# Attention plus feed-forward on one core: a four-sum seven-product form, reciprocals kept in PSUM, GpSimd casts in quarters, other PSUM rings, and stores issued by ScalarE

## The chip, the cores and the metric

The kernel runs on 1 core of one Trainium2 chip. The metric is device microseconds of one execution; lower is better. A profiled execution also has a span, from its first to its last instruction, which lies some 2 us under its time.

In the profile's lines PE is TensorE, DVE VectorE, ACT ScalarE, POOL GpSimd and SP SyncE; a q behind the name (SPq) means its queue of issues, and L194 is line 194 of the kernel. Tiles named _ps lie in banks of PSUM, one of the chip's two kinds of on-chip memory used here, and take TensorE's products; all other tiles lie in SBUF, the other kind.

## The reference, cut to what matters

There are two softmax attentions in a row, then a feed-forward layer whose weights serve all batches. 512 of the 576 tokens of a batch are "main" tokens; the other 64 are the "remainder", which the kernel collects over four batches into one "remainder unit".

```python
# q, k, v: (8 batches, 8 heads, 576, 64); p: (8, 8, 32, 64)
p_packed = softmax(p @ k.T / 8) @ v             # 32 packed rows per head
out      = softmax(q @ p_packed.T / 8) @ p_packed
x = out.transpose(0, 2, 1, 3).reshape(4608, 512)
h = x @ w_in                                    # 512 -> 2048
g = h * sigmoid(beta * h)
y = g @ w_out                                   # 2048 -> 512
```

## The kernel before

The program orders itself: every piece of work is a task with an engine, a duration, its dependencies and a rank, and a planner lays the tasks out in time once, when the program is built. The order found is fixed in each engine's queue. In the tile names, h_ps, o_ps and w_ps are PSUM banks of h, of the output and of a batch's fused weights W_bf (p_packed times w_in, scaled; h is then one product of the second softmax with them); hr_ps is h of the remainder; g_main is g, which ScalarE makes with the activation called silu here.

For one output unit (256 tokens by 512 outputs) `g @ w_out` is done as seven products of half blocks instead of eight. VectorE makes the sums, TensorE the products into four PSUM banks, ScalarE and VectorE gather them in `o_sb`, and SyncE stores them:

```python
# sums: 3 instructions, 5 blocks of 128x1024
S[0:2] = g[0:2] + g[2:4];  S[2] = g[0] + g[3];  g[1:3] = g[1:3] - g[0:4:3]
# banks: C = A11*w3 | A22*w4,  D = S5*w5 | S2*w2,  A = S7*w7 | S6*w6,  B = S1*w1
# takes: copy of C on ScalarE, then subtract D, add D, add A, add B on VectorE
...
def store(self, unit):
    if unit[0] != "r":                                   # main unit: one store
        nc.sync.dma_start(rows[:, 2 * v : 2 * v + 2, :], o[:])
    else:                                                # remainder unit: four
        for e in range(4):
            nc.sync.dma_start(self.out[lo : lo + SR, :], o[64 * (e % 2) : ..., e // 2, :])
```

The second softmax's sums are inverted by ScalarE as exp(-ln z), out of PSUM into an SBUF tile `rz2`, from which VectorE multiplies:

```python
nc.scalar.activation(rz[:, i, 0:SM], ps[:], AF.Ln)       # PSUM -> SBUF
nc.scalar.activation(rz, rz, AF.Exp, scale=-1.0)         # in SBUF
nc.vector.tensor_tensor(A2T, E2T, rz, ALU.mult)
```

The rings of PSUM banks are 2 for h, 3 for the output, 3 for attention.

The softmax here doesn't subtract the row's maximum and nothing guards it: scores larger than these inputs give would overflow.

## Time and profile before

| | before |
|---|---|
| time, median of 3 runs | 261.63 us (261.55 to 262.82) |
| span of the profiled execution, granted clock | 259.1 us, 0.998 |
| TensorE, VectorE, ScalarE, GpSimd busy | 93, 77, 68, 24% |

The profiled execution took 260.84 us, less than all three timed runs.

This is the timeline of SyncE (start, length, queue, line, operation, count):

```profile
167.79 1.27 SPq L250 DMA_DIRECT2D k32r<-in_k_dram  x2
169.10 0.61 SPq L242 DMA_DIRECT2D v<-in_v_dram  x1
169.81 2.56 SPq L809 DMA_DIRECT2D out_dram<-o_sb  x4
```

The view of waits (who waited for whom: total us, times, longest) says that stores hold this queue for long, and that silu (L639) hardly ever holds TensorE:

```profile
SPq L805 <- DVE o_sb L782: 55.5, 7, 14.3
...
PE h_ps L194 <- ACT g_main L639: 0.6, 3, 0.2
```

A store at the head of SyncE's queue waits for VectorE's last addition, up to 14.3 us, and all loads behind it wait too. That is what moving the stores to another engine aims at. SyncE computes nothing, so its waiting only matters when a load becomes late.

### The profile page before, as it was taken

To read this page: it belongs to the slowest core of one execution; us is meant where nothing else is said; L and a number is where in the kernel's file an instruction comes from. 1 tells how busy PE (TensorE), PEld (TensorE's weight loads), DVE (VectorE), ACT (ScalarE), POOL (GpSimd) and SP (SyncE) were. 2 spreads that over 40 slices of the span, in tenths; PEclk is the share of its full clock that TensorE was granted. 3 is DMA by queue.
4 is the path that set the end of the run, shared out by engine and by line. 5 is a ranking of instruction groups with operands and counts; after the bars stand their busy time and mean duration, and the time that the engine had idled before them with its cause. 6 is when DMAs were issued, how large, how long until landed. Compare 5 with 4: busy or idle time off the path is not lost.

```text
span 259.1 us, 6793 instructions
## 1 busy us (share of the span) xinstructions
PE 241.7 (93%) x2897; PEld 193.8 (75%) x2897; DVE 199.2 (77%) x288; ACT 176.1 (68%) x308; POOL 63.4 (24%) x58
## 2 busy tenths in 40 slices
PE   4899689899989999998999999999999999999990
PEld 4897576566554878886778877877889778889880
DVE  6476766887985987796888968979996688665771
ACT  1153579867877878879786987886898768765000
POOL 4320433151440741342315231600900000000000
PEclk9999999999999999999999999999999999999999
DMA  7999999997998998996998999989660102201113
GB/s 225 352 320 268 280 325 384 348 330 183 288 199 237 292 246 235 212 333 148 265 251 263 143 318 291 205 227 272 174 172 7 79 0 83 82 27 60 81 81 81
DMA packets 73471, 54.18 MB, mean 209 GB/s; under 512 B 42065, under 2 KB 66657, under 8 KB 73441
## 3 DMA queue, kind: packets, MB, share of 16 engines
q1 hardware_dynamic: 73440, 53.76, 75.2%
q8 instruction: 22, 0.36, 0.6%
q14 instruction: 9, 0.07, 0.1%
HBM read 37.23 MB, written 9.44 MB: 180 GB/s over the span
## 4 chain that ended last, share of the span: by engine, by line
PE 56%; DMA 20%; SPq 10%; ACT 4%; issue 3%; POOL 3%; DVE 2%; POOLq 0%
PE o_ps L194 31%; PE h_ps L194 14%; DMA k<-in_k_dram 9%; SPq L336 5%; DMA v<-in_v_dram 4%; PE w_ps L194 3%; DMA qT<-q_bf 3%; SPq L250 2%; PE hr_ps L194 2%; DMA q32r<-in_q_dram 2%; DMA v32r<-in_v_dram 2%; PE z_ps L194 2%; PE s_ps L194 1%; SPq L242 1%; ACT g_main L639 1%
## 5 line engine op out<-in xcount | busy, mean ns | idle before, releaser
L639 ACT ACTIVATE g_main<-h_ps 128x512 bf16<-128x512 f32 x128 | 71.1, 596 | 29.5 <-PE h_ps L194 28.6
L194 PE MATMUL h_ps<-A2T,W_bf 128*128 128x256 bf16 x512 | 70.2, 273 | 0.6 <-ACT g_main L639 0.6
L194 PEld LDWEIGHTS <-W_bf 128*128 128x128 bf16 x768 | 57.1, 98 | 12.7 <-issue 4.7
L194 PE MATMUL o_ps<-w_mix,g_main 128*128 128x256 bf16 x448 | 59.5, 273 | 0.0
L194 PEld LDWEIGHTS <-g_main 128*128 128x128 bf16 x512 | 48.2, 98 | 12.5 <-issue 2.9
L600 DVE TENSOR_TENSOR W_bf<-w_ps,beta_bc 128x512 bf16<-128x512 f32 x64 | 41.5, 682 | 5.7 <-PE w_ps L194 5.2
L194 PEld LDWEIGHTS <-g_sums 128*128 128x128 bf16 x384 | 36.4, 98 | 5.5 <-issue 1.4
L209 ACT ACT_TABLE_LOAD x28 | 35.9, 1283 | 1.2 <-PEq L1067 0.7
L194 PE MATMUL o_ps<-w_out_bf,g_sums 128*128 128x256 bf16 x256 | 33.9, 273 | 0.0
L707 DVE TENSOR_TENSOR g_sums<-g_main 128x2048 bf16<-128x2048 bf16 x14 | 21.8, 1555 | 4.8 <-ACT g_main L639 4.8
L194 PE MATMUL warm_ps<-identr 128*128 128x128 bf16 x256 | 21.9, 237 | 3.7 <-DVE bones L858 3.7
L276 POOL CAST q_bf<-q 128x2048 bf16<-128x2048 f32 (+1 forms) x7 | 14.6, 2081 | 33.5 <-DMA q<-in_q_dram 19.9
L194 PEld LDWEIGHTS <-identr 128*128 128x128 bf16 x256 | 18.0, 108 | 5.5 <-DVE bones L858 3.7
L276 POOL CAST v_bf<-v 128x2048 bf16<-128x2048 f32 (+1 forms) x7 | 13.4, 1912 | 26.2 <-PE h_ps L194 9.8
L774 DVE TENSOR_TENSOR o_sb<-o_sb,o_ps 128x512 f32<-128x512 f32 x16 | 11.0, 685 | 10.0 <-ACT g_main L639 2.5
L541 DVE TENSOR_TENSOR A2T<-E2T,rz 128x512 bf16<-128x512 bf16 (+1 forms) x24 | 13.6, 587 | 5.5 <-ACT rz L536 5.5
L276 POOL CAST k_bf<-k 128x2048 bf16<-128x2048 f32 (+1 forms) x7 | 12.4, 1771 | 21.4 <-DMA k<-in_k_dram 10.4
L711 DVE TENSOR_TENSOR g_main<-g_main 128x2048 bf16<-128x2048 bf16 x14 | 17.4, 1244 | 0.0
L194 PE MATMUL o_ps<-w_mix,g_sums 128*128 128x256 bf16 x128 | 17.3, 273 | 0.0
L194 PE MATMUL o_ps<-w_out_bf,g_main 128*128 128x512 bf16 x64 | 17.0, 380 | 0.0
L772 ACT COPY o_sb<-o_ps 128x512 f32<-128x512 f32 x16 | 9.4, 588 | 10.3 <-PE o_ps L194 10.2
L194 PEld LDWEIGHTS <-pp 64*32 64x32 bf16 x384 | 6.0, 88 | 13.5 <-issue 10.9
(86 smaller groups left out, 296.5 us busy)
## 6 DMA issues: line engine op xcount, KB each, us to landing
out_dram<-o_sb SPq DMA_DIRECT2D x16, 512.0 KB, 3.9
k<-in_k_dram SPq DMA_DIRECT2D x7, 1024.0 KB, 8.5
v<-in_v_dram SPq DMA_DIRECT2D x7, 1024.0 KB, 6.8
q<-in_q_dram SPq DMA_DIRECT2D x7, 1024.0 KB, 6.7
w_in<-in_moe_w_in_dram SPq DMA_DIRECT2D x4, 1024.0 KB, 9.4
w_out<-in_moe_w_out_dram SPq DMA_DIRECT2D x4, 1024.0 KB, 12.4
k<-in_k_dram SPq DMA_DIRECT2D x2, 512.0 KB, 5.4
k32r<-in_k_dram SPq DMA_DIRECT2D x16, 64.0 KB, 5.2
```

The source lines that it names most:

```text
L194: return self.nc.tensor.matmul(out, lhsT, rhs, start=start, stop=stop, tile_position=pos, skip_group_check=True)
L209: self.nc.scalar.preload_act_table_set(SETS[mode])
L250: nc.sync.dma_start(t[64 * g : 64 * g + 64, :].rearrange("p (h d) -> p h d", h=4), src[b, 4 * g : 4 * g + 4, SM:S, :].rearrange("h p d -> ...
L276: self.copy[engine](self.t[b, x][:, 0:2048].rearrange("p (t h d) -> p h t d", t=4, h=8)[:, h], self.t[b, x, "32"][:].rearrange("p (h t d) ...
L336: nc.sync.dma_start_transpose(t[:], st[b, x][:])
L541: nc.vector.tensor_tensor(part(st[b, "A2"], i), part(st[b, "E2"], i), part(st[b, "rz2"], i), ALU.mult)
L600: nc.vector.tensor_tensor(st[b, "W"][:, r, cols], st[b, "w", m][:], self.beta_bc[:, cols], ALU.mult)
L639: nc.scalar.activation(st[b, v, "g"][:, :, f, :], st[b, "h", v, f][:].rearrange("p (q n) -> p q n", q=4), AF.Silu)
L707: nc.vector.tensor_tensor(st[*unit, "S"][:, 0:2], g[:, 0:2], g[:, 2:4], ALU.add)
L711: nc.vector.tensor_tensor(g[:, 1:3], g[:, 1:3], g[:, 0:4:3], ALU.subtract)
L772: nc.scalar.copy(middle, st[*unit, "C"][:])
L774: nc.vector.tensor_tensor(ends, middle.rearrange("p (h n) -> p h n", h=2)[:, ::-1], halves(st[*unit, "D"]), ALU.subtract)
```

## The change

It has seven parts: (1) four sums and seven products that accumulate in two banks, with reads in the middle; (2) the second softmax's reciprocals stay in PSUM; (3) the first softmax's reciprocal is applied per partition, to the exponent and to W_bf; (4) GpSimd casts in pieces of 128x512; (5) PSUM rings 3 for h, 2 for output, 3 for attention; (6) q of the first two batches has staging of its own; (7) the first 16 units are stored by ScalarE, and the planner's order is retuned with 1119 per-task offsets. Besides, one unit instead of two is done with plain products, and the second remainder unit now comes before the last main unit.

In the diff, cut to its core, the lines of sums, steps, casts and reciprocals are condensed.

```diff
+STORE_US = 5.0
+STORE = 'ACT'
+RINGS = {'h': 3, 'o': 2, 'att': 3}
+OFFSETS = {0: 10.1, 1: 4.7, 2: 101.3, ...}              (1119 entries, cut)
...
     def add(self, engine, us, fn, deps=(), rank=0, ...):
+        rank += OFFSETS.get(len(self.tasks), 0)
...
-                self.copy[engine](to, of)
+                m = 2 if engine == "POOL" else n
+                for j in range(0, n, m):
+                    self.copy[engine](to[:, j : j + m], of[:, j : j + m])
...
-            nc.scalar.activation(rz[:, i, 0:SM], ps[:], AF.Ln)
-            nc.scalar.activation(rz, rz, AF.Exp, scale=-1.0)
-            nc.vector.tensor_tensor(A2T, E2T, rz, ALU.mult)
+            nc.scalar.activation(sums(i), sums(i), AF.Ln)
+            nc.scalar.activation(sums(i), sums(i), AF.Exp, scale=-1.0)
+            nc.vector.tensor_tensor(A2T, E2T, sums(i), ALU.mult)
...
+        0: S0 = a21 + a22;  1: S1 = S0 - a11;  2: S2 = a12 - S1;  3: a21 = a11 - a21
+        steps = a21*B21 -> bank 1, a11*B11 -> bank 0, S0*T1 -> bank 1, S1*T2 -> bank 0,
+                S2*B22 -> bank 1, a12*T3 -> bank 0, a22*T4 -> bank 0    (a take between two)
...
+    def plan_store(self, unit, deps):
+        e = STORE if len(self.outs) < 17 else "SP"
+        us = {"POOL": 1.0, "ACT": 0.5, "SP": 1.5}[e]
+        self.task(("store", unit), e, us, lambda: self.store(unit, e), deps, -10)
+
-    def store(self, unit):
+    def store(self, unit, engine):
+        dma = {"POOL": self.nc.gpsimd, "ACT": self.nc.scalar, "SP": self.nc.sync}[engine].dma_start
```

The planner takes a store on ScalarE for 0.5 us of that engine. Here the store of the first remainder unit, four transfers, is among the 16 units that ScalarE stores.

## The prediction

> **What bounds the kernel now.** I read, in this order, the page's busy row and slices, the stretches of 10 us, the chain, and the timelines of the start and of the end.
>
> ```profile
> PE 241.7 (93%) x2897; PEld 193.8 (75%) x2897; DVE 199.2 (77%) x288; ACT 176.1 (68%) x308; POOL 63.4 (24%) x58
> ...
> DMA  7999999997998998996998999989660102201113
> ```
>
> TensorE (PE) looks like the bound, but the ends of matmuls are modelled, so I take its pace from the chain:
>
> ```profile
> 198.27 3.06 PE o_ps L194 x28
> ...
> 237.83 15.30 PE o_ps L194 x140
> ```
>
> Both lines (start, length, what) give 0.109 us for a matmul of 128x256. In the same way a 512-wide one of the plain output takes 0.218 us (two in 0.43), an hr_ps one 0.029 (32 in 0.93), a w_ps one 0.043 (eight in 0.34), a pp_ps one 0.029 (20 in 0.58). With these I weigh all matmuls of the built program, fillers (warm_ps, identity products that only keep PE busy) left out: 212.7 us of real work in a span of 259.1. The other 46.4 us are what can be won. Where are they? The timelines show:
>
> ```profile
> 46.13 0.41 PE L194 MATMUL w_ps<-w_in_bf,pp 64*32 64x512 bf16 x8
> ...
> 44.49 1.59 POOL L975 CAST w_in_bf<-w_in 128x1024 bf16<-128x1024 f32 x1 [1.26 <-DMA w_in<-in_moe_w_in_dram]
> ```
>
> At 46.13 PE starts the last column block of batch 0's fused weights, which needs the last quarter of w_in, landed at 44.49 and cast until 46.08. I use this as the anchor. Before it PE does 212.7 - 197.2 = 15.5 us of real work, so 30.6 us of the 46.4 lie there, spent on loads. After it 197.2 us of work are left (488 h and 896 output products of 0.109 = 150.7; 64 plain of 0.218 = 13.9; small ones 32.6) and PE ends at about 253.15, 207.0 later: 9.8 us of gaps, of which stretch counts put about 2.8 before 60, 4.1 between 60 and 130, and 2.5 after that. The last 5.9 us are the end:
>
> ```profile
> 253.15 0.69 DVE L782 TENSOR_TENSOR o_sb<-o_sb,o_ps 128x512 f32<-128x512 f32 x1 [0.19 <-PE o_ps L194]
> 253.87 2.46 SPq L809 DMA_DIRECT2D out_dram<-o_sb  x4
> ```
>
> One addition, then four stores issued one after the other, and their landing.
>
> The start is a matter of loads. SyncE's queue (SPq) issues them in order, and it stood still twice:
>
> ```profile
> 13.11 1.06 SPq L242 DMA_DIRECT2D q<-in_q_dram  x1
> 19.26 0.37 SPq L242 DMA_DIRECT2D k<-in_k_dram  x1
> 19.73 1.28 SPq L250 DMA_DIRECT2D k32r<-in_k_dram  x2
> 21.05 1.27 SPq L250 DMA_DIRECT2D q32r<-in_q_dram  x2
> 22.73 0.37 SPq L242 DMA_DIRECT2D v<-in_v_dram  x1
> 28.08 0.37 SPq L242 DMA_DIRECT2D q<-in_q_dram  x1
> ```
>
> Nothing is issued from 14.2 to 19.26 and from 23.1 to 28.08, because k, v and q share two staging buffers. In the stretches the rate is 324, 255, 336 and 379 GB/s from 10 to 50 us: the dip from 20 to 30 follows these stops.
>
> **What the Trainium skill says.** "TensorE: Matmul & The Clock Gate", section "Back-to-back issue gap", gives 262 cycles at 2.4 GHz for 256 columns, which is 109 ns: the trace agrees. The same section's sustained 131 ns for 512 columns does not hold here, 218 ns does. "SBUF — State Buffer", section "Who interferes with whom", says that a VectorE instruction with two SBUF inputs contends with a GpSimd instruction that reads SBUF. The trace agrees:
>
> ```profile
> 85.42 1.89 POOL L276 CAST v_bf<-v 128x2048 bf16<-128x2048 f32 x1 [9.76 <-PE h_ps L194]
> ...
> 85.69 2.69 DVE L707 TENSOR_TENSOR g_sums<-g_main 128x2048 bf16<-128x2048 bf16 x1
> ```
>
> The sum takes 2.69 us beside a cast, and 1.22 after 190 us, where GpSimd is idle. "PSUM — Partial Sum Buffer", section "The four PSUM rules", allows a synchronised read of a partial sum in the middle of an accumulation; the new form lives on that, and no run of before shows it. "DMA: Bandwidth & Descriptors", section "Issuing engines are not separate DMA queues", says that issuing from another engine saves only sequencer time, so I count nothing for stores on ScalarE (ACT) as transfers.
>
> **The change part by part.**
>
> PE: only the first unit of outputs stays plain instead of two. 32 matmuls of 0.218 = 6.97 become 56 of 0.109 = 6.10: -0.9 us. The first softmax's sums are 80 products with one moving column; I estimate 0.029 each, the pace at which hr_ps loads weights, against 0.040 now: -0.9 us. Total work 210.8 against 212.7. But the order of the built program, counted from the same anchor, leaves 197.7 us after it (492 and 952 of 0.109 = 157.3; 32 of 0.218 = 7.0; 33.4 small), not less than 197.2: batch 1's q is loaded after w_in now, so its transposes and scores, and some h, move behind the anchor. The saved PE work therefore shows only in front, where PE idles anyway. This is the central step: **PE work after the anchor: +0.5 us.**
>
> Loads: q of batches 0 and 1 gets its own staging, so k and v of batch 1 wait only for the casts of k and v of batch 0. Counted from the SyncE order, about 12.1 MiB stand up to the last w_in, against 12.2 before. If the stretch from 20 to 30 us moves at the neighbours' 330 GB/s instead of 255, it carries 0.75 MB more, worth 2.3 us. The cast behind it goes in two halves of estimated 0.6. **Anchor: -2 us.**
>
> VectorE (DVE): the sums become four of 128x1024 (0.685 each beside an idle GpSimd) for 17 units, 46.6 us, against 61.2 now (21.8 + 17.4 + 15.8 + 6.2 for the remainder units). With GpSimd's casts in quarters a sum meets at most about 0.6 us of cast, not 1.89, so I add some 4 us. The 128x128 reciprocals fall from 8 x 0.952 to 8 x about 0.16 (-6.3). The normalisation falls from 16 x 0.287 to 8 x about 0.42 (-1.2). One w_mix operation less: -1.3. Evictions: 102 of 128x256 at an estimated 0.42 (0.685 less the 256 columns at 0.96 GHz) = 42.8, against 43.6 + 2.7. W_bf gets a second factor: 64 x 0 to 0.06 = up to +3.8. Sum: 199 to about 179. DVE isn't the bound, so this is worth only shorter gaps.
>
> ACT: 16 copies of 0.588 become 17 of about 0.38 (-3), and 19 store issues come on its queue, at the 0.6 that one costs on SPq (+11). Both kernels load 28 tables. ACT stays near 75%; the danger is that a store at its head waits for an eviction and holds up silu.
>
> Buffers: three banks for h let PE run one product further ahead of silu, which aims at the handshake near 50 us, where ACT and PE alternate with 0.2 us waits. Two for o with reads in the middle of accumulations mean that two steps on the same bank need an eviction between them, about 0.2 + 0.42 + 0.2; another step of 8 x 0.109 = 0.87 fits into this, except before the last unit's last step: +0.7. The reciprocals hold their bank for some 2 us. I expect **gaps: -2.5 us** of the 9.8, mainly before 130 us, and **tail: -0.4 us**: +0.7 as said, and -1.1 because the last unit is now a main one, with one store instead of four.
>
> Sum: +0.5 - 2 - 2.5 - 0.4 = -4.4. As the order was retuned task by task, which works on exactly these gaps, I lean 1 us further: 261.6 - 5.4 = 256.2.
>
> **Rivals.**
>
> (1) The anchor doesn't move. Loads are in flight in nearly every slice up to 190 us, the same bytes are wanted, and the two stops may be hidden by the backlog. For it: 1.05 to 1.09 of DMA share. Against: the dip to 255 GB/s. Then 258 to 260.
>
> (2) A new wait eats the gain. Batch 1's q arrives behind w_in and w_out, and its softmax comes after batch 0's silu; PE has 17.4 us of listed work between the anchor and batch 1's first h, against my count for ACT of 13 silus (7.2), a table load (1.3) and a softmax (5 to 6) with its hops: just enough. If PE has to wait there, or stores block ACT, the result is 259 to 263.
>
> (3) The gaps nearly vanish and the loads come faster still: gaps at 4 us and the anchor at 43 make 259.1 - 3.1 + 0.5 - 5.8 - 0.4 = 250.3 of span, 252.8 as time (the median lies 2.5 above the span). For it: after 130 us the old order already loses only 2.5 us in 123.
>
> **Range and chances.** The sum's terms are uncertain by about 2 us (anchor), 2.5 (gaps) and 1 (tail, stalls), together some 3.4 us: 8 in 10 within 251.3 to 260.8. The 2% line is at 256.4, just above my number, so faster by over 2% and the same are close; slower than 266.9 would take a new serial wait of 10 us, for which I see nothing.
>
> **What would show it.** Right: last w_in cast ending near 44 instead of 46.08; PE's last product near 249; gaps of some 7 us after the anchor; 128x1024 sums near 0.75 on average; one store after the last addition; DVE near 180 us busy. Wrong: the anchor at 46 or later (loads), PE waits named ACT or a q transfer between 50 and 65 us (rival 2), or matmul pace other than 0.109 in the unit products because they wait on evictions.

## The result, and the profile after

| | before, same rounds | after |
|---|---|---|
| median | 262.14 us, 4 runs | 269.06 us, 4 runs (268.44 to 271.89) |
| ratio, 95% interval | | 1.0284 (1.0205 to 1.0363): slower |
| span and clock of the profiled execution (before: the earlier one) | 259.1 us, 0.998 | 267.3 us, 0.987 |

A ratio is the mean time of one kernel's fast runs over that of the other's fast runs of the same rounds, so it isn't quite the ratio of the medians beside it. Executions over 1.5% slower than the fastest of the same kernel are left out of the means.

The page of the changed kernel: busy row, then three rows of 40 slices (6.7 us each).

```profile
PE 242.8 (91%) x2915; PEld 196.9 (74%) x2915; DVE 176.9 (66%) x335; ACT 172.9 (65%) x309; POOL 70.2 (26%) x119
...
PE   4988789999799999999999999099999999999992
...
ACT  1136544863998897998798984094898898653000
...
PEclk9999999999999999999999999869999999999999
```

In slice 25 (counted from 0: 167 to 174 us) both TensorE and ScalarE show 0, and the granted clock drops to 8 and then 6 tenths in this slice and the next. One hole, not a general slowness. ScalarE's timeline across it (in brackets: how long the engine was idle before, and what ended it):

```profile
162.80 0.60 ACT L749 ACTIVATE g_main<-h_ps 128x512 bf16<-128x512 f32 x1
168.41 4.66 ACTq L919 DMA_DIRECT2D out_dram<-o_sb  x4
173.11 1.57 ACT L749 ACTIVATE g_main<-h_ps 128x512 bf16<-128x512 f32 x3 [9.72 <-DMA q<-in_q_dram]
```

ScalarE's last silu ends at 163.40. Then the four stores stand at the head of its queue: the first goes out at 168.41, the last at 172.59, and only then silu goes on. The bracket doesn't name an eviction by VectorE, it names the load of q. SyncE's timeline has that load and the ones before it:

```profile
160.51 1.42 SPq L365 DMA_DIRECT2D v32r<-in_v_dram  x2
162.02 1.38 SPq L365 DMA_DIRECT2D k32r<-in_k_dram  x2
164.82 0.37 SPq L357 DMA_DIRECT2D q<-in_q_dram  x1
```

Why should a store of o_sb wait for a load of q? The built program says it. Every transfer issued by SyncE or ScalarE reports its landing on one of eight semaphores (counters that instructions can wait for), which the build hands out in program order across both queues, and before an issue a queue waits until the transfer that had this semaphore last has landed. For the four stores:

```
store   semaphore   had it last (issued by SyncE)   waits besides for
1       DMAHW0      v32r, second half               VectorE's take
2       DMAHW1      k32r, first half                -
3       DMAHW2      k32r, second half               VectorE's take
4       DMAHW3      q, 1 MB                         -
```

VectorE's takes are not what held them: the two named in the table had ended at 161.43 and 164.96 in the trace, before ScalarE was free for the first store (163.40) and before the third one's turn (169.59). The chain of waits confirms the last row to 0.02 us (start, length, what):

```profile
164.82 7.75 DMA q<-in_q_dram
172.57 0.02 issue
172.59 0.47 ACTq L919
...
175.20 1.71 PE o_ps L295 x8
...
177.33 1.59 PE hr_ps L295 x32
```

The q load is issued at 164.82 and lands 7.75 us later, at 172.57; the fourth store goes out at 172.59. The last two lines show a second cost: eight matmuls of 128x256 take 1.71 us, 0.214 each instead of 0.109, and 32 hr_ps 1.59 us instead of 0.93. After its idle time TensorE is granted a mean clock of 0.66 in the 10 us from 170 on.

The Trainium skill states both halves of this. "DMA: Bandwidth & Descriptors", section "Anatomy of one DMA — SWDGE (gpsimd) path", a section on GpSimd's transfers, notes that "any semaphore wait happens on the issuing sequencer before dispatch", and "Perfetto Trace Analysis", section "Tensor Engine Instruction (MATMUL, LD_WEIGHTS)", notes that "ACT/DVE/GPSIMD are strict FIFO". The trace agrees with both: 9.72 us during which silus wait behind a store.

TensorE's timeline at the anchor, at the hole, and at the end:

```profile
44.73 0.96 PE L295 MATMUL w_ps<-w_in_bf,pp 64*32 64x512 bf16 x8 [0.27 <-POOL w_in_bf L1088]
...
173.76 1.01 PE L295 MATMUL h_ps<-A2T,W_bf 128*128 128x256 bf16 x4 [6.62 <-ACT g_main L749]
...
261.92 1.03 PE L295 MATMUL o_ps<-w_mix,g_main 128*128 128x256 bf16 x8 [0.51 <-DVE o_sb L877]
```

I count TensorE's gaps in the way of the prediction, as a stretch less its matmuls at their paces. The third column is the first experiment, below, in which only those four stores are back on SyncE:

| stretch | before | after | rem_sp |
|---|---|---|---|
| anchor to 60 us | 2.8 | 1.8 | 2.4 |
| 60 to 75 | 0.7 | 2.3 | 2.4 |
| 75 to 150 | 4.1 | 3.5 | 3.3 |
| 150 to 190 | 1.2 | 10.1 | 1.2 |
| 190 to TensorE's end | 0.9 | 2.9 | 2.6 |
| sum | 9.7 | 20.5 | 11.7 |

Of the 10.1 us from 150 to 190, 6.62 are the wait itself; 1.5 more are the low clock behind it, in the two groups just shown (1.71 and 1.59 us instead of 0.87 and 0.93). A part of the change that works as intended is seen in the groups of instructions (count, busy us, mean ns, then idle time before):

```profile
L830 DVE TENSOR_TENSOR g_sums<-g_main 128x1024 bf16<-128x1024 bf16 x15 | 11.1, 737 | 2.6 <-ACT g_main L749 2.1
```

The sums meet short casts only: 737 ns on average for this form. Before, one of 128x2048 took 2.69 us beside a long cast and 1.22 without.

### The profile page after: what moved, and what is told of

Same layout as the page of the kernel before. It is cut to its first block, busy times and chain, and to the rows that moved or that the text cites.

```text
span 267.3 us, 6970 instructions
## 1 busy us (share of the span) xinstructions
PE 242.8 (91%) x2915; PEld 196.9 (74%) x2915; DVE 176.9 (66%) x335; ACT 172.9 (65%) x309; POOL 70.2 (26%) x119
## 4 chain that ended last, share of the span: by engine, by line
PE 58%; DMA 22%; SPq 6%; DVE 5%; POOL 3%; issue 2%; ACT 1%; ACTq 1%; POOLq 0%; DVEq 0%
PE o_ps L295 32%; PE h_ps L295 16%; DMA w_out<-in_moe_w_out_dram 6%; DMA w_in<-in_moe_w_in_dram 4%; DMA qT<-q_bf 4%; SPq L365 3%; DMA q<-in_q_dram 3%; DMA v32r<-in_v_dram 3%; PE hr_ps L295 3%; PE w_ps L295 3%; DMA k<-in_k_dram 2%; PE s_ps L295 2%; SPq L357 2%; PE z_ps L295 1%; SPq L1076 1%
## 5 line engine op out<-in xcount | busy, mean ns | idle before, releaser
L710 DVE SCALAR_TENSOR_TENSOR W_bf<-w_ps,rz,beta_bc 128x512 bf16<-128x512 f32 x64 | 45.3, 744 | 21.4 <-PE w_ps L295 21.3
L295 PE MATMUL o_ps<-w_out_bf,g_main 128*128 128x256 bf16 (+1 forms) x272 | 39.2, 285 | 0.9 <-DVE o_sb L879 0.5
L877 DVE TENSOR_TENSOR o_sb<-o_sb,o_ps 128x256 f32<-128x256 f32 x51 | 21.2, 418 | 24.1 <-PE o_ps L295 23.5
L295 PE MATMUL o_ps<-w_mix,g_sums 128*128 128x256 bf16 x272 | 36.6, 277 | 0.2
L295 PE MATMUL o_ps<-w_mix,g_main 128*128 128x256 bf16 x240 | 33.1, 273 | 0.5 <-DVE o_sb L877 0.5
L879 DVE COPY o_sb<-o_ps 128x256 f32<-128x256 f32 x51 | 21.3, 420 | 16.8 <-PE o_ps L295 15.1
L395 POOL CAST q_bf<-q 128x512 bf16<-128x512 f32 x26 | 17.3, 706 | 46.0 <-DMA q<-in_q_dram 25.3
L395 POOL CAST k_bf<-k 128x512 bf16<-128x512 f32 x26 | 15.8, 652 | 21.2 <-DMA k<-in_k_dram 13.9
L395 POOL CAST v_bf<-v 128x512 bf16<-128x512 f32 x26 | 16.8, 686 | 11.6 <-PE h_ps L295 3.1
L295 PE MATMUL o_ps<-w_out_bf,g_sums 128*128 128x256 bf16 x136 | 18.8, 273 | 0.0
```

The costliest lines, as they stand in the source:

```text
L295: return self.nc.tensor.matmul(out, lhsT, rhs, start=start, stop=stop, tile_position=pos, skip_group_check=True)
L395: self.copy[engine](to[:, j : j + m], of[:, j : j + m])
L710: nc.vector.scalar_tensor_tensor(st[b, "W"][:, r, cols], st[b, "w", m][:], st[b, "rz1"][:, r : r + 1], self.beta_bc[:, cols], ALU.mult, AL ...
L877: nc.vector.tensor_tensor(o, o, ps, ALU.add)
L879: self.copy[engine](o, ps)
```

## The experiments

The theory (A) after the first reading: the time is lost because the four remainder stores wait on ScalarE for SyncE's loads, and silu with them. The rivals: (1) it is the change of store engine as a whole, wherever the stores stand; (2) the new arithmetic and buffers have made something else slower. All kernels gave correct results. This is the overview; "before" is measured again in each batch.

| run | median us of its fast runs | ratio to before | 95% interval |
|---|---|---|---|
| rem_sp | 258.94 | 0.9866 | 0.9790 to 0.9942 |
| rem_sp_again | 259.42 | 0.9914 | 0.9861 to 0.9968 |
| rem_pool | 260.65 | 0.9965 | 0.9874 to 1.0055 |
| rem_two | 265.19 | 1.0079 | 0.9997 to 1.0160 |
| before_rem_act | 270.50 | 1.0329 | 1.0277 to 1.0381 |
| before_all_act | 271.68 | 1.0323 | 1.0232 to 1.0413 |
| all_sp | 265.43 | 1.0102 | 1.0008 to 1.0196 |
| all_pool | 272.84 | 1.0367 | 1.0290 to 1.0444 |
| rem_sp_prime | 259.85 | 0.9901 | 0.9810 to 0.9993 |
| rz_sbuf | 264.30 | 1.0096 | 1.0023 to 1.0169 |
| whole | 260.20 | 0.9922 | 0.9869 to 0.9975 |
| untuned | 266.21 | 1.0170 | 1.0115 to 1.0226 |

### rem_sp: the four stores back on SyncE

```diff
     def store(self, unit, engine):
+        engine = "SP" if unit[0] == "r" else engine
```

> The changed kernel in its planned order, only the four stores of the first remainder unit are issued by SyncE instead of ScalarE. Theory A: these four stores stood at the head of ScalarE's queue from 163.4 to 173.1 us, waiting on DMA semaphores held by SyncE's loads (the last one by a 1 MB load of q), and so held up silu and PE. Then the wait of 9.7 us on ScalarE and the PE gap of 6.6 us vanish: 259 to 261 us. Theory B: batch 7's k and q land late and PE would starve there whatever issues the stores: 266 us or more. DMA bytes and PE work are the same in both.

258.94 us, just under what I expected; the profiled execution has span 258.0, clock 0.995. The same three silus now start at 165.29 instead of 173.11, and the stores go out on SyncE at 172.22:

```profile
165.29 1.57 ACT L749 ACTIVATE g_main<-h_ps 128x512 bf16<-128x512 f32 x3 [1.92 <-PE h_ps L295]
...
172.22 3.40 SPq L920 DMA_DIRECT2D out_dram<-o_sb  x4
```

TensorE loses 1.2 us between 150 and 190 instead of 10.1, and nothing else was touched. One added line makes the difference between 2.8% slower and 1.3% faster than before (0.9% in the second measurement, rem_sp_again).

### before_rem_act: the remainder's stores moved alone, in the kernel before

```diff
-                nc.sync.dma_start(self.out[lo : lo + SR, :], o[64 * (e % 2) : ..., e // 2, :])
+                nc.scalar.dma_start(self.out[lo : lo + SR, :], o[64 * (e % 2) : ..., e // 2, :])
```

> The kernel before with nothing but the two remainder units' stores (four each) issued by ScalarE at their old places; main stores stay on SyncE. Theory A (the four stores at the head of ScalarE's queue wait for SyncE's loads that went eight transfers earlier, and silu with them): a wait of ScalarE of 3 us or more near 168 to 173, a PE gap of 3 to 4.5 us behind it, and 265 to 267 against some 262.5. Theory B (it is the main stores on ScalarE that cost the time in before_all_act): within 1 us of before, and no such wait.

270.5 us: 8 us lost by one word, more than expected. The word moves the second remainder unit's four stores too; the loss is at the first unit's: TensorE's gaps from 150 to 190 are some 9 us larger than before. ScalarE's and TensorE's timelines:

```profile
166.41 5.53 ACTq L809 DMA_DIRECT2D out_dram<-o_sb  x4
171.98 1.08 ACT L639 ACTIVATE g_main<-h_ps 128x512 bf16<-128x512 f32 x2 [8.78 <-DMA k32r<-in_k_dram]
...
172.63 1.01 PE L194 MATMUL h_ps<-A2T,W_bf 128*128 128x256 bf16 x4 [7.87 <-ACT g_main L639]
```

Again the bracket names a load. It is the last of four waits: by the issues and landings in the trace the first store waited for a main store of SyncE (landed at 166.33), the second for a transposition (169.70), the other two for halves of k32r (the last landed at 171.44). VectorE's last addition had ended at 161.98, before ScalarE's wait began at 163.2. None of the new arithmetic and none of the new buffers is in this kernel, so rival (2) isn't needed for the loss.

### before_all_act: all stores on ScalarE, in the kernel before

```diff
-            nc.sync.dma_start(rows[:, 2 * v : 2 * v + 2, :], o[:])
+            nc.scalar.dma_start(rows[:, 2 * v : 2 * v + 2, :], o[:])
     (and the four of the remainder as in before_rem_act)
```

> The kernel before in its order, with all stores issued by ScalarE instead of SyncE: one part of the change alone. Theory A: ScalarE's head waits on SyncE's loads through the shared DMA semaphores; silu and PE stop as in the changed kernel: 266 to 275 us, with waits of ScalarE of several us in front of its stores. Rival: ScalarE is busy only 68% and takes stores without harm, 261 to 263 us, and the loss of the changed kernel needs its new order.

271.68 us, as theory A expected. Its ratio, 1.0323, is that of before_rem_act, 1.0329. TensorE waits 4.43 us at 174.13, behind the remainder's stores, and 3.07 us at 125.80, behind a main store that waited on ScalarE for a load of k32r. So a main store can be held in the same way; the sum isn't larger than with the remainder's alone.

### rem_two: two stores for the four

```diff
+            rows = self.out.rearrange("(b s) n -> s b n", s=S)[SM:S, 4 * unit[1] : 4 * unit[1] + 4]
+            if unit[1] == 0:
+                for r in range(2):
+                    dma(rows[:, r::2, :], o[64 * r : 64 * r + 64, :, :])
+                return
```

> The changed kernel with the first remainder's four stores on ScalarE as it has them, but merged into two. In the built program the two wait only on the DMA semaphores DMAHW0 and DMAHW1, which in the changed kernel's trace were free at 168.4 and 169.0 us; the third and fourth, which waited for 169.9 and for the 1 MB load of q until 172.6, are gone. Theory A (each store waits for the DMA that used its semaphore last): ScalarE is released some 3.5 us earlier, the wait falls from 9.7 to about 6 us, 265 to 266.5 us. Rival (ScalarE waits for the evictions of the unit or for the issue of the stores itself): released at about the same time or one issue earlier, 268 to 269 us.

With two stores only two semaphores are needed. ScalarE goes on at 169.84 instead of 173.11:

```profile
169.84 1.57 ACT L749 ACTIVATE g_main<-h_ps 128x512 bf16<-128x512 f32 x3 [6.69 <-DVE g_main L830]
...
170.49 0.78 PE L295 MATMUL h_ps<-A2T,W_bf 128*128 128x256 bf16 x4 [3.27 <-ACT g_main L749]
```

The bytes stored are the same, the wait is 6.69 us instead of 9.72, and the time is about 3.9 us shorter (medians of different batches); the expectation of theory A held. The bracket names VectorE, whose work only happened to end last before silu: the first store went out at 168.44, when the second half of v32r had landed at 168.37, and the second was issued until 169.80. What sets the wait is which earlier transfer each store has to see landed, not the size of the stores.

### rem_pool: the four stores on GpSimd

```diff
+        engine = "POOL" if unit == ("r", 0) else engine
```

> The changed kernel with the first remainder unit's four stores issued by GpSimd at the same place of the plan, all else as it is; GpSimd's stores use semaphores of their own in the built program and wait only for VectorE's evictions. Theory A (ScalarE's wait was for SyncE's loads, through the shared semaphores): no wait of ScalarE near 163 to 173, PE gap there under 1 us, and 258.5 to 261, as in rem_sp. Theory B (four stores at this place cost the time on any queue of a computing engine): GpSimd's casts come late, k's transposition and the next batch's scores with them, a PE gap of 3 us or more between 165 and 200, and 264 or more.

In the built program GpSimd's stores have semaphores of their own. Its timeline:

```profile
169.85 0.40 POOL L398 CAST k_bf<-k32r 128x256 bf16<-128x256 f32 x1 [5.73 <-DMA k32r<-in_k_dram]
170.40 2.20 POOL L920 DMA_DIRECT2D out_dram<-o_sb  x4
```

The stores go out even at 170.40, behind a cast that waits for its load, and cost nothing: TensorE loses 1.0 us between 150 and 190. The median of its three fast runs, 260.65, lies in the 258.5 to 261 expected, and the profiled span is 258.5, beside 258.0 of rem_sp. Theory B of this run fails. With so few runs the interval holds 1: that this version beats before isn't shown.

### all_sp: all stores on SyncE

```diff
+        engine = "SP"
```

> As the last one, but all stores are issued by SyncE, order of the plan kept. Theory A: as without the four stores, and the first store on ScalarE, which took 3.5 us to issue, is gone too: 257 to 260 us. Rival: SyncE now stands at its head until evictions are done (it did for 55 us in the kernel before), loads and transposes come later, and new PE gaps open: 262 to 266 us.

My expectation failed, the rival's range held: 265.43. Main stores on SyncE do wait at the head for VectorE (60.2 us in nine waits). But the longest waits of TensorE are not for late loads. VectorE's and TensorE's timelines show one:

```profile
114.86 0.42 DVE L879 COPY o_sb<-o_ps 128x256 f32<-128x256 f32 x1 [2.81 <-DMA out_dram<-o_sb]
...
115.33 1.03 PE L295 MATMUL o_ps<-w_mix,g_sums 128*128 128x256 bf16 x8 [2.21 <-DVE o_sb L879]
```

A store that SyncE issued at 105.33 landed 9.4 us later, at 114.76, and until then VectorE couldn't write that o_sb again. In rem_sp ScalarE issued this store at 104.67, and it landed after 5.1 us. TensorE's wait of 2.20 us at 171.18 is of the same kind (8.3 us to land). Why a store lands later from SyncE's queue, no run settles. So this order, which was made for stores on ScalarE, is slower without the 15 main stores there, and faster only without the remainder's.

### all_pool: ScalarE's stores on GpSimd

```diff
+        engine = "POOL" if engine == "ACT" else engine
```

> All stores that ScalarE issues in the changed kernel are issued by GpSimd at the same places of the plan. The built program shows that these stores have semaphores of their own (DMASW) and wait for evictions alone. Theory A: no wait of ScalarE or PE near 163 to 173 us, time as with the four stores on SyncE, 257.5 to 260 us. Rival 1: GpSimd's casts stand behind stores that wait for evictions, so k and q are late and PE waits for transposes: 261 to 265 us. Rival 2: the loss near 167 us is due to late loads after all: 266 us or more.

272.84 us. Theory A and rival 1 failed; the time lies in the range of rival 2, but not for its reason. The wait near 163 to 173 is gone, but the timelines of GpSimd, VectorE and TensorE show another one earlier:

```profile
143.86 0.53 POOL L916 DMA_DIRECT2D out_dram<-o_sb  x1
...
149.17 0.43 DVE L879 COPY o_sb<-o_ps 128x256 f32<-128x256 f32 x1 [9.02 <-DMA out_dram<-o_sb]
...
149.65 1.01 PE L295 MATMUL o_ps<-w_mix,g_sums 128*128 128x256 bf16 x4 [8.43 <-DVE o_sb L879]
```

The store stands in GpSimd's queue behind the casts of k, which began at 141.63 after 3.38 us of waiting for k. It goes out at 143.86, lands at about 149.1, and only then VectorE may write that o_sb again, and TensorE the PSUM bank. It is the mirror of the first case: a queue that waits for loads makes stores late, as a store that waits makes a queue late.

### rem_sp_prime: an earlier first transfer on ScalarE's queue

In rem_sp too, ScalarE's first store is strange; every other one takes 0.34 to 0.40 us (where this store is the first transfer on ScalarE's queue, the other runs of the new kernel show 3.2 to 4.8):

```profile
63.34 3.53 ACTq L916 DMA_DIRECT2D out_dram<-o_sb  x1
```

The edit issues beta's load from ScalarE at the very start:

```diff
+        self.b16 = self.const.tile([16, 128], f32, name="b16")
+        nc.scalar.dma_start(self.b16[:], self.beta.rearrange("(f p) -> f p", p=128))
...
-            nc.sync.dma_start(self.b16[:], self.beta.rearrange("(f p) -> f p", p=128))
```

> The four stores on SyncE, and beta's small load moved to ScalarE's queue at the very start, so that this queue's first DMA is no longer a store at 63 us. If the 3.5 us of that first issue belong to the first use of the queue: the issue at the start takes the 3.5 us while ScalarE has nothing to do, the first store takes 0.34 us, and the time falls 1.5 to 3 us below the run without it (257 to 259). If the 3.5 us are a wait on a load: the first store still takes over 2 us and the time is the same within 1 us.

The long issue disappears (0.37 us at 63.56; beta's at the start takes 0.40, not 3.5), but the time doesn't fall: TensorE then waits 1.88 us at 69.99 for k's transposition. And in before_all_act the first store of ScalarE took 0.38 us without any such preparation. So what makes it 3.5 us stays open, and taking it away alone gained nothing.

### rz_sbuf: the reciprocals in SBUF again

```diff
-            nc.scalar.activation(sums(i), sums(i), AF.Ln)
+            if i == 0:
+                st[b, "rz2"] = self.one.tile([128, 2, S], f32, tag="rz2", name="rz2")
+            nc.scalar.activation(part(st[b, "rz2"], i), sums(i), AF.Ln)
     (the exponential and the product from rz2 too; on top of rem_sp)
```

> The four stores on SyncE, and the reciprocals of the second softmax's sums written to SBUF as in the kernel before instead of staying in PSUM. One part undone, order kept. Expected: ScalarE's exponentials on them go from about 580 to 630 ns, the product A2T on VectorE contends with GpSimd's casts again (0.69 to about 0.74 us), both off the path: within 1 us of the run without it (258 to 260 us). If the part is worth something by itself, 261 us or more.

A miss: 264.3, where I expected rem_sp's time within 1 us. The same stores of ScalarE, found in both timelines, show where it comes from: the second is 1.2 us later than in rem_sp, the seventh (144.52 against 143.60) 0.9 later, the eighth (160.46 against 157.31) 3.2 later, the last 3.9 later. So up to the eighth store the part costs the expected 1 us. The chain has the step at the eighth:

```profile
151.62 8.77 DMA kT<-k_bf
160.38 0.02 issue
160.40 0.02 ACTq L919
```

This store has to wait until k's transposition has landed, which had the store's semaphore last. It is the theory's wait once more, now in a main store: ScalarE was free at 158.36 and VectorE's take was done at 158.03, so the wait is 2.0 us of the 4.0 by which the spans differ (262.0 against 258.0). The store then lands at 168.13, and VectorE and TensorE (1.48 us at 169.03) wait for that. Why the transposition is issued over 6.79 us here and 3.99 in rem_sp, I couldn't settle.

### whole: GpSimd's casts uncut

```diff
-                m = 2 if engine == "POOL" else n
+                m = n
     (and w_in's cast in one piece; on top of rem_sp)
```

> The four stores on SyncE, and GpSimd's casts whole again instead of in quarters. Expected: the 128x1024 sums on VectorE rise from 0.74 us on average to about 0.9, GpSimd's busy time falls by some 8 us, PE's gaps change little: 258 to 260 us. If the quarters matter for PE, the gaps after 60 us grow by 2 us or more: 261 us or more.

The time, 260.2, is as expected. The sums get longer on the whole, though less than I wrote (means of 813, 690 and 794 ns against 727, 739 and 719 in rem_sp), GpSimd is 57.6 us busy against 71.8, VectorE 180.3 against 177.1. The medians differ from the two of rem_sp by 1.3 and 0.8 us; that the quarters are worth anything isn't shown.

### untuned: without the table of offsets

```diff
-        rank += OFFSETS.get(len(self.tasks), 0)
```

> rem_sp (the changed kernel with the first remainder unit's four stores on SyncE) with the table of about 1200 per-task offsets left out, so that the planner orders the same instructions by its own ranks. Theory A, the prediction's step: the retuning is worth about 1 us beside the change's own parts, so this takes 259.5 to 261.5 and is still about 0.5 to 1% faster than before. Theory B: what rem_sp gains over before is the tuned order, and the parts by themselves bring little: then 263 or more, with new PE gaps of 2 us and over in the trace, at waits that rem_sp doesn't have.

266.21 us: my step was too small, theory B held. Without the table the same instructions take 6.8 us more (median) than in rem_sp_again of the same batch. TensorE's largest wait falls behind ScalarE's first store:

```profile
70.97 1.32 PE L294 MATMUL h_ps<-A2T,W_bf 128*128 128x256 bf16 x8 [3.12 <-ACT g_main L748]
```

The gaps from 60 to 75 are 5.2 us (2.4 in rem_sp), and all those after 75 add up to 11.4 (7.0 in rem_sp).

### rem_sp_again: the best version in five rounds

> rem_sp once more, unchanged, in five rounds. If it beats the kernel before by what the first measurement showed, the ratio lies at 0.983 to 0.991 with an interval that excludes 1; if that was a chance of three rounds, the interval reaches 0.995 or more.

The ratio is 0.9914, at the edge of what I wrote, and the interval (0.9861 to 0.9968) excludes 1 but not 0.995. This kernel beats before and the changed kernel. Over both measurements the gain against before is about 1%, less than the 2% that count as faster.

Not run: the new form with the old rings of 2, 3 and 3 banks. With the table of offsets the planner finds no order for it; without the table it builds, and could have been compared with untuned. So what the rings bring by themselves stays open, as does the new form against the old with all else equal.

## Why the prediction was wrong

**The step that failed** is the one on ScalarE: "19 store issues come on its queue, at the 0.6 that one costs on SPq (+11) ... the danger is that a store at its head waits for an eviction and holds up silu". The cost of an issue was even overstated: most took 0.34 us. The danger was seen, but the cause of the wait was looked for in the wrong place: evictions account for none of it. The four stores of the first remainder unit wait for the landing of four loads of SyncE, up to 7.75 us after issue, because the built program's eight semaphores are shared by both queues. For this ScalarE stood 9.72 us and TensorE 6.62. rem_sp, before_rem_act, rem_two and rem_pool show it from four sides; in before_rem_act the four waits were for a store, a transposition and two loads of SyncE. It could have been read before the run: the changed kernel can be built, and each store's waits stand in the built program. I looked only at the order of the instructions.

**The reading of the skill.** "I count nothing for stores on ScalarE (ACT) as transfers" was right for the bytes and led astray for the queue. Rival (2) did name "or stores block ACT", with 259 to 263. The blocking was shown, at 269. The sentence on a slowdown over 266.9, "would take a new serial wait of 10 us, for which I see nothing", came near the size: the wait is 9.72 us on ScalarE. The reading of the matmul page was too narrow: beside the 131 ns that don't hold, the same section gives 518 cycles for 512 columns, 216 ns, which do.

**The anchor** was expected 2 us earlier and came 1.4 us earlier (46.13 to 44.73; 44.66 in rem_sp). But part of this is the cast in halves: the first two of the eight products now start after the first half. Like with like, the last w_in cast ends at 45.24 instead of 46.08 (predicted: near 44) and starts at 43.54 instead of 44.49, so the loads brought 0.9 us, under half of the step. Nor does it come from the stretch named: from 20 to 30 us the rate rose from 255 to 301 GB/s, but from 10 to 20 it fell from 324 to 273, so as much was moved by 30 us (8.6 MB) in both kernels. The gain is between 30 and 40 (380 GB/s against 336), and SyncE still issued nothing from 27.1 to 33.7 and from 34.6 to 39.3.

**TensorE's work after the anchor** was taken as +0.5, 197.7 us. The matmuls in the trace of after, weighed with the same paces from the anchor to TensorE's end, add up to 197.8. The step held.

**The gaps** were to fall by 2.5 and rose by 10.8 (9.7 to 20.5). 8.9 of this is the stretch from 150 to 190. The rest is a second error, in the step on gaps: in rem_sp, without the wait, gaps are 11.7, so they rose by 2.0. Two places gave back more than the stretches up to 60 and from 75 to 150 won (-1.2): 60 to 75 us, where ScalarE's first store takes 3.5 us, and the last stretch, +1.6 each before rounding; in the latter the wait for a bank before the last step is 0.51, against 0.7 foreseen. That the long first store causes the first of these was only argued: taking it away brought another wait (rem_sp_prime).

**The tail** was better than said: from TensorE's end to the end of the span 5.95 us before, 4.35 after. A single store is worth 1.6 us, not 1.1.

**The lean of 1 us for the retuned order** was mis-sized: leaving the offsets out costs 6.8 us. This is not the retuning against the old order, which had ranks tuned for its own tasks; it says that the new parts without their tuned order would be slower than before.

**VectorE** came out as worked out: 176.9 us busy against about 179, sums near 0.74 us, evictions 0.42, and no run shows that this bought anything by itself. ScalarE was 65% busy instead of "near 75%", as the page doesn't count issues as busy.

With the four stores on SyncE the sum becomes +0.2 (197.5 us of work counted in its trace against 197.3 in that of before) - 1.5 + 2.0 - 1.8 (tail 4.15) = -1.1, and the spans do differ by 259.1 - 258.0 = 1.1. The two profiles are a fast execution of before and the slowest of the four of rem_sp, so this is too small a gain: the ratios of all fast runs say 0.9 to 1.3%, some 2.3 to 3.5 us. Even so the predicted -4.4 of the parts, and -5.4 with the lean, was too hopeful, and in these two profiles it is the step on gaps that missed most (+2.0 instead of -2.5).

## What to carry to other kernels

Before you move a transfer to the queue of a computing engine, list for the built program everything its issue waits for, not only its data: which earlier transfer had its semaphore, on which queue that stands, and when it lands. An instruction that may wait at the head of an in-order queue costs as much as the work behind it is urgent, so put each store where the waiting hurts least: here, in this order, main stores on ScalarE and remainder stores on SyncE. And a fix of the order has to be judged together with its plan: the same instructions took 6.8 us more without the tuned order.

## What the Trainium skill lacked or had wrong

- "DMA: Bandwidth & Descriptors", section "Issuing engines are not separate DMA queues": it counts only the saved sequencer time. Here one store word moved to ScalarE cost 8 us, since the issue waited (9.72 us after, 8.78 in before_rem_act) for transfers of SyncE with the same semaphores. The page says that an issue can wait on its sequencer, but no page that I looked up says that a built program may hand out few completion semaphores to all queues in turn, and so tie a store to transfers that it has nothing to do with; here there were eight.
- "TensorE: Matmul & The Clock Gate", section "Back-to-back issue gap": its sustained 131 ns for 512 columns isn't reached, 218 ns is. Its table, which it calls the gap of an isolated matmul, agrees with streams of them here: 262 cycles (109 ns) for 256 columns and 518 (216 ns) for 512.
- "PSUM — Partial Sum Buffer", section "The four PSUM rules": a synchronised read in the middle of an accumulation gave correct results in all runs. The page has no cost for it; here TensorE waited 0.51 us before the last step, where no other work lay between.
- "SBUF — State Buffer", section "Who interferes with whom": the rule agrees, and here are sizes for one product, which it lacks. With the reciprocals read from SBUF (rz_sbuf) the product A2T of 128x512 took 875 ns on average when GpSimd worked beside it and 687 when not; with them in PSUM (rem_sp) 679 and 683.
- None that I looked up gives such a long first issue on ScalarE's queue: 3.53 us in rem_sp, then 0.34; and 0.38 in another program, so it isn't simply the first use. Its cause is open.
